# One load for the last heads' output weights in a fused decode layer: all 12 rows per partition behind the last V

## Chip, cores, metric

One core of a Trainium2 chip. The metric is the device time in microseconds; a traced execution's span is some 2 us shorter than its time. A run here means one timed execution. In the profiles PE is TensorE's matmuls and PEld its weight loads, DVE is VectorE, ACT ScalarE, POOL GpSimd, and SP the engine that issues most loads. The granted clock is the share of full speed that PE was given.

## The reference

Attention of one query position over the last 2048 cached positions, for 2 batch entries and 32 heads of 192, then a gated feed-forward layer. Almost every byte read is used once.

```python
q = (layernorm(x) @ wq)                                  # 640 -> 32 heads x 192
p = softmax(q . k_cache[:, :, 6144:, :] * 192 ** -0.5)
h = x + (p . v_cache[:, :, 6144:, :]) @ wo               # 6144 -> 640
h2 = h + (gelu(layernorm(h) @ w_gate) * (layernorm(h) @ w_up)) @ w_down
```

## The kernel before

SP issues every large load in one order into a ring of six slots; a load is issued when the work on what its bytes overlap is done. The last eight heads (J = 3) use wo in three pieces: 8 and 3 rows per partition through the ring, and the last 128 rows of wo through a separate early load `wosp` on ACT's queue, ahead of x.

```python
P.op("act", lambda e: e.dma_start(wosp[32:96, :, :], A_wo[WOE:, :].rearrange("(p j) n -> p j n", j=2)), W=["wosp"], dma="dsp")
P.op("act", lambda e: e.dma_start(xrow[0:2, :], A_x[:, 0, :]), W=["xrow"], dma="dx")
load_k(0)
load_wq()
# ... K and V of 16 groups, wo of J = 0 and 1 between them (cut)
load_wo(2)
load_wo(3)
load_ffn()                      # gate, up (2 parts), w_down (4 parts of 6, 3, 2, 1 rows)

def wo_parts(J):
    return ((0, 12),) if J < 3 else ((0, 8), (8, 11))

# the end of the program
pv(15)
o_rows(3)
oproj(2)
o_columns(3)
oproj(3)                        # wosp's rows, then 8 rows, then 3: 4 + 16 + 6 matmuls of 320 columns
h_columns()                     # then layernorm, gate, up, down
```

Of the kernel before, what the change touches and what calls it, by code (L numbers as in the profile page):

```python
# [5 lines left out]
BF16 = mybir.dt.bfloat16  # L6
F32 = mybir.dt.float32
I32 = mybir.dt.int32
ALU = mybir.AluOpType
ACT = mybir.ActivationFunctionType  # L10
AX = mybir.AxisListType

B = 2
D = 640
NC5 = D // 128
HQ = 32
DH = 192
# [198 lines left out]
RING = 6 * SLOT  # L216
TPG = 64
WDC = ((0, 6), (6, 9), (9, 11), (11, 12))
WOE = 6016
WUC = ((0, 4), (4, 5))  # L220
BIG = 1.0e9
K_AT = (0, SLOT, 3 * SLOT, 5 * SLOT)
# [6 lines left out]
def bass_sequential_preLN__sliding_block_cached__geglu_ffn__decode_kernel(  # L229
# [12 lines left out]
    with ExitStack() as ctx:  # L242

        def sb(name, shape, dt):
            return ctx.enter_context(nc.sbuf_tensor(name, shape, dt))

        def ps(name, shape, dt):
            return ctx.enter_context(nc.psum_tensor(name, shape, dt))
# [5 lines left out]
        identf = sb("identf", [128, 128], F32)  # L254
# [12 lines left out]
        selb = sb("selb", [128, 2], BF16)  # L267
# [4 lines left out]
        pf = sb("pf", [128, 11], F32)  # L272
        pg = sb("pg", [128, 13], F32)
        ci = sb("ci", [128, 128], I32)
        cti = sb("cti", [128, 4, 128], I32)
        cf = sb("cf", [128, 5, 128], F32)
        ei = sb("ei", [128, 6], I32)
        ef = sb("ef", [128, 6], F32)
        ge = sb("ge", [128, 6, 5], F32)

        wosp = sb("wosp", [128, 2, D], BF16)
        xrow = sb("xrow", [128, D], BF16)
        xT = sb("xT", [128, NC5, B], F32)
        ls = sb("ls", [128, 2, B], F32)
# [12 lines left out]
        sm = sb("sm", [128, 512], F32)  # L297
# [7 lines left out]
        ering = sb("ering", [128, 4, 32, 32], BF16)  # L305
        osb = sb("osb", [128, 384], F32)
        orow = sb("orow", [128, 8, DH], BF16)
        ot = sb("ot", [128, 13, B], BF16)
        yrow = sb("yrow", [128, 160], BF16)
        hrow = sb("hrow", [128, 320], F32)  # L310
        hsel = sb("hsel", [128, 2, 17], F32)
        grow = sb("grow", [128, 384], F32)
        urow = sb("urow", [128, 384], F32)
        gsb = sb("gsb", [128, NF * B], F32)
        ga = sb("ga", [128, 4, NF * B], F32)
        uT = sb("uT", [128, NF, 18], BF16)
# [1 line left out]
        tps = [ps(f"tps{i}", [128, 512], F32) for i in range(4)]  # L318
        sps = ps("sps", [128, 512], F32)
        ops_ = ps("ops", [128, 512], F32)  # L320
        m1 = ps("m1", [128, 512], F32)
        m2 = ps("m2", [128, 512], F32)

        P = _Prog()
# [4 lines left out]
        def load(key, off, nbytes, src, shape, sem):  # L329
            queue.append((key, off, nbytes, src, shape, sem))  # L330
# [16 lines left out]
        def done(*keys):  # L347
            used.update(keys)
            pump()
# [13 lines left out]
                 lambda v: v.rearrange("p (c n) -> p c n", n=HQ * DH), "wq")  # L363

        def load_wo(J):
            nk = 12 if J < 3 else 11
            src = A_wo[1536 * J:1536 * J + 128 * nk, :].rearrange("(p kk) n -> p kk n", kk=nk)
            for i, (k0, k1) in enumerate(wo_parts(J)):
                load(("wo", J, i), WO_AT[J] + 2 * k0 * D, 2 * (k1 - k0) * D, src[:, k0:k1, :],
                     lambda v: v.rearrange("p (kk n) -> p kk n", n=D), "wo" if J < 2 else f"wo{J}{i}")  # L370

        def wo_parts(J):
            return ((0, 12),) if J < 3 else ((0, 8), (8, 11))

        def load_ffn():
            load(("wg", 0), K_AT[1], 2 * NC5 * F, B_w_gate.rearrange("(p c) f -> p c f", c=NC5),
# [11 lines left out]
        def dve(fn, R=(), W=(), X=(), cls=1):  # L388
            return P.op("dve", fn, R, W, X, cls=cls)

        def act(fn, R=(), W=(), X=()):
            return P.op("act", fn, R, W, X)

        def pe(fn, R=(), W=(), X=()):
            return P.op("pe", fn, R, W, X)

        def pool(fn, R=(), W=(), X=()):
            return P.op("pool", fn, R, W, X)
# [7 lines left out]
        def tt(out, a, b, op):  # L406
            return lambda e: e.tensor_tensor(out=out, in0=a, in1=b, op=op)  # L407

        P.op("act", lambda e: e.dma_start(wosp[32:96, :, :], A_wo[WOE:, :].rearrange("(p j) n -> p j n", j=2)), W=["wosp"], dma="dsp")
        P.op("act", lambda e: e.dma_start(xrow[0:2, :], A_x[:, 0, :]), W=["xrow"], dma="dx")  # L410
        load_k(0)
        load_wq()
# [18 lines left out]
        pool(lambda e: e.memset(ering[:, :, :, :].rearrange("p a b c -> p (a b c)").bitcast(I32), 0), W=[("er", k) for k in range(4)])  # L431

        pool(lambda e: e.memset(uT[:, :, :].rearrange("p a b -> p (a b)").bitcast(I32), 0), W=["uT"])
        pool(lambda e: e.memset(wosp[0:32, :, :].rearrange("p a b -> p (a b)").bitcast(I32), 0), W=["wosp0"])

        dve(lambda e: e.tensor_copy(cf[:, 0, :], ci[:, :]), R=["ci"], W=["cf0"])
        dve(lambda e: e.tensor_copy(pg[:, 0:1], pi[:, :]), R=["pi"], W=["row"])
# [32 lines left out]
        def _x_T(e):  # L470
# [11 lines left out]
            R=["pi"] + [("bits", k) for k in range(11)], W=["pti"])  # L482
# [205 lines left out]
                   wm[:, :].unsqueeze(2).to_broadcast([128, 8, DH]), ALU.mult), R=["wm"], W=["orow"], X=[tok])  # L688

        def o_columns(J):  # L690
            nk = 12 if J < 3 else 11
            of = orow[:, :, :].rearrange("p h d -> p (h d)")

            def fn(e):
                for kk in range(nk):
                    ins = e.matmul(m2[:, 2 * kk:2 * kk + 2], lhsT=of[:, kk:128 * nk:nk], rhs=selb[:, :], start=True, stop=True)  # L696
                for j in range(13 - nk if J == 3 else 0):
                    ins = e.matmul(m2[0:96, 22 + 2 * j:24 + 2 * j], lhsT=of[:, 128 * nk - 64 + j:1536:2], rhs=selb[:, :], start=True,
                                   stop=True)
                return ins  # L700

            pe(fn, R=["orow", "selb"], X=["m2"])
            n = 24 if J < 3 else 26
            dve(lambda e: e.tensor_copy(ot[:, :, :].rearrange("p k b -> p (k b)")[:, 0:n], m2[:, 0:n]), W=["ot"], X=["m2"])

        def oproj(J):
            def fn_early(e):
                for j in range(2):
                    for h in range(2):
                        r = 2 * j + h  # L710
                        ins = e.matmul(m1[32 * r:32 * r + 2, 192:512], lhsT=ot[0:96, 11 + j, :], rhs=wosp[0:96, j, 320 * h:320 * (h + 1)],
                                       start=False, stop=False, tile_position=(0, 32 * r), skip_group_check=True)
                return ins

            if J == 3:
                pe(fn_early, R=["wosp", "wosp0", "ot"], X=["m1"])
            for i, (k0, k1) in enumerate(wo_parts(J)):
                wo, wtoks = where["wo", J, i]

                def fn(e, k0=k0, k1=k1, wo=wo):  # L720
                    if J == 2:
                        for h in range(2):
                            e.matmul(m1[32 * h:32 * h + 2, 192:512], lhsT=identb[0:2, 0:2], rhs=xrow[0:2, 320 * h:320 * (h + 1)],
                                     start=True, stop=False, tile_position=(0, 32 * h), skip_group_check=True)
                    for kk in range(k0, k1):
                        for h in range(2):
                            r = 2 * (kk % 2) + h
                            ins = e.matmul(m1[32 * r:32 * r + 2, 192:512], lhsT=ot[:, kk, :],  # L728
                                           rhs=wo[:, kk - k0, 320 * h:320 * (h + 1)], start=(kk == 1 or J < 2 and kk == 0) and J < 3,
                                           stop=(J < 2 and kk >= 10 or J == 3 and kk >= 9), tile_position=(0, 32 * r), skip_group_check=True)  # L730
                    return ins

                pe(fn, R=wtoks + ["ot", "xrow", "identb"], X=["m1"])
                done(("wo", J, i))
            if J == 0:
                dve(lambda e: e.tensor_copy(hrow[0:98, :], m1[0:98, 192:512]), W=["hrow"], X=["m1"])
            if J == 1:
                dve(tt(hrow[0:98, :], m1[0:98, 192:512], hrow[0:98, :], ALU.add), R=["hrow"], W=["hrow"], X=["m1"])
            if J == 3:
                dve(lambda e: e.tensor_tensor_reduce(out=hrow[0:98, :], in0=m1[0:98, 192:512], in1=hrow[0:98, :], scale=1.0, scalar=0.0,  # L740
                                                     op0=ALU.add, op1=ALU.add, accum_out=rs[0:98, :]), R=["hrow"], W=["hrow", "rs"], X=["m1"])
# [69 lines left out]
        def ffn_columns(row, tok, bank, i):  # L811
            def fn(e):
                for j in range(3):
                    ins = e.transpose(bank[:, 128 * j:128 * j + 98], row[0:98, j:384:3], identf[0:98, 0:98])
                return ins

            pe(fn, R=[tok, "identf"], X=[("t", i)])
            return bank[:, 0:384].rearrange("p (j r y) -> p r j y", j=3, y=32)[:, :, :, 0:2]

        def h_rows(e):  # L820
# [6 lines left out]
            return t.rearrange("p (r j b) -> p r j b", r=4, j=3)  # L827

        ffn_in(sps, "s", "wg", ((0, NC5),))
        dve(lambda e: e.tensor_copy(grow[0:98, :], sps[0:98, 0:384]), W=["grow"], X=["s"])  # L830
        pe(h_rows, R=["hrow", ("hsel", 0), ("hsel", 1)], X=["m1"])
        gT = ffn_columns(grow, "grow", tps[0], 0)
        dve(lambda e: e.tensor_copy(rjb(gsb[:, :]), gT), W=["gsb"], X=[("t", 0)])
        dve(tt(ga[:, 0, :], gsb[:, :], gsb[:, :], ALU.mult), R=["gsb"], W=["ga0"])
        dve(ts(ga[:, 1, :], ga[:, 0, :], 0.044715, ALU.mult, 1.0, ALU.add), R=["ga0"], W=["ga1"])
# [3 lines left out]
        dve(lambda e: e.reciprocal(ga[:, 1, :], ga[:, 3, :]), R=["ga3"], W=["ga1"])  # L839
        dve(tt(ga[:, 0, :], ga[:, 1, :], gsb[:, :], ALU.mult), R=["ga1", "gsb"], W=["ga0"])  # L840
        ffn_in(ops_, "o", "wu", WUC)
        act(lambda e: e.activation(out=urow[0:98, :], in_=ops_[0:98, 0:384], func=ACT.Copy), W=["urow"], X=["o"])
        vT = ffn_columns(urow, "urow", tps[1], 1)
        dve(tt(uT[:, :, 0:17:16].rearrange("p (r j) b -> p r j b", r=4), vT, rjb(ga[:, 0, :]), ALU.mult), R=["ga0"], W=["uT"], X=[("t", 1)])
        for i, (f0, f1) in enumerate(WDC):
            wd, wtoks = where["wd", i]

            def fn(e, f0=f0, f1=f1, wd=wd):
# [10 lines left out]
             dma="dout")  # L859
# [59 lines left out]
```

## Time and profile before

| | before |
|---|---|
| time, median of 3 (lowest to highest) | 294.46 us (294.35 to 294.63) |
| span of the traced run | 292.5 us |
| bytes moved | 122.44 MB in 6586 packets |
| mean granted PE clock | 0.857 |

The table is read together with the lines shown in the prediction below: full transfer engines, and a PE that waits for the last loads.

### The profile page before, as it was taken

How to read it: one execution, taken by the hardware profiler on the slowest of the kernel's cores; microseconds unless marked ns; L12 is line 12 of the kernel's file. 1: busy time of each engine (PE TensorE's matmuls, PEld its weight loads, DVE VectorE, ACT ScalarE, POOL GpSimd, SP SyncE). 2: the span in 40 equal slices, each digit the busy share in tenths (PEclk: the TensorE clock that was granted, in tenths of full speed). 3: DMA queues.
4: the chain of work that ended last, by engine and by line, in shares of the span. 5: the costliest groups of instructions: out<-in, count | busy, mean ns of one | idle time of the engine just before them, and what ended most of it. 6: DMA issues, size and time to landing. Idle time of an engine off the chain costs nothing.

```text
span 292.5 us, 5073 instructions
## 1 busy us (share of the span) xinstructions
PE 194.5 (66%) x2144; PEld 152.3 (52%) x2144; DVE 128.4 (44%) x310; ACT 96.2 (33%) x120; POOL 9.2 (3%) x37
## 2 busy tenths in 40 slices
PE   0248568848778198849496596759596957585674
PEld 0238356717465195628283575457566744563432
DVE  4186165623537154616155154425365554262321
ACT  1023134623442143616142153325252543341000
POOL 4000010000000000000000000000000000000000
PEclk9995989995979579998869599969797999897955
DMA  7999999999999999999999999999999999999993
GB/s 280 442 437 421 426 430 430 429 429 430 426 434 421 434 430 431 430 430 430 434 427 428 434 430 430 430 434 430 430 434 434 430 430 430 430 430 415 422 412 148
DMA packets 6586, 122.44 MB, mean 419 GB/s; under 512 B 750, under 2 KB 880, under 8 KB 1584
## 3 DMA queue, kind: packets, MB, share of 16 engines
q1 hardware_dynamic: 6480, 122.13, 97.8%
q8 instruction: 7, 0.11, 0.2%
q10 hardware_dynamic: 96, 0.17, 0.1%
q14 instruction: 3, 0.02, 0.0%
HBM read 122.29 MB, written 0.00 MB: 418 GB/s over the span
## 4 chain that ended last, share of the span: by engine, by line
DMA 77%; PE 19%; SPq 2%; DVE 1%; issue 0%
DMA ring<-in_A_k_cache_dram 57%; PE tps L558 15%; DMA ring<-in_A_wq_dram 10%; DMA ring<-in_B_w_down_dram 10%; SPq L345 2%; PE tps L579 1%; PE ops L660 1%; PE m L728 1%; PE m L696 1%; DVE ktr L570 0%; DVE ering L407 0%; PE m L851 0%; PE m L644 0%; PE m L674 0%; DVE yrow L857 0%
## 5 line engine op out<-in xcount | busy, mean ns | idle before, releaser
L558 PE MATMUL tps<-identf,ring 128*128 128x128 f32 x768 | 116.5, 321 | 46.8 <-DMA ring<-in_A_k_cache_dram 41.5
L558 PEld LDWEIGHTS tps<-identf,ring 128*128 128x128 f32 x768 | 108.1, 169 | 49.9 <-DMA ring<-in_A_k_cache_dram 42.7
L567 ACT ACTIVATE ktr<-tps 128x1024 bf16<-128x1024 bf16 x80 | 79.4, 1023 | 87.3 <-PE tps L558 87.3
L570 DVE COPY ktr<-tps 128x1024 bf16<-128x1024 bf16 x112 | 74.2, 688 | 75.1 <-PE tps L558 74.3
L635 ACT ACTIVATE eexp<-sm,nm 128x512 bf16<-128x512 f32 x16 | 11.5, 721 | 65.4 <-DVE nm L633 65.4
L660 PE MATMUL ops<-ring,ering 128*32 128x384 bf16 x512 | 25.0, 339 | 6.1 <-DMA ring<-in_A_v_cache_dram 6.1
L624 DVE CUSTOM_DVE_ANT_1 sm<-sps,mska 128x512 f32<-128x512 f32 x16 | 11.1, 692 | 36.0 <-PE sps L616 36.0
L616 PE MATMUL sps<-ktr,rq 128*16 128x512 bf16 x384 | 24.6, 388 | 1.1 <-POOL rq L407 1.1
L660 PEld LDWEIGHTS ops<-ring,ering 128*32 128x32 bf16 x512 | 12.7, 99 | 14.9 <-DMA ring<-in_A_v_cache_dram 7.6
L616 PEld LDWEIGHTS sps<-ktr,rq 128*16 128x16 bf16 x384 | 9.3, 88 | 11.4 <-POOL rq L407 1.2
L631 PEld LDWEIGHTS m<-mrhs,pm 128*128 128x128 bf16 x16 | 1.5, 96 | 23.4 <-DVE mrhs L403 23.4
L631 PE MATMUL m<-mrhs,pm 128*128 128x16 bf16 x16 | 2.9, 183 | 15.8 <-DVE mrhs L403 15.8
L407 POOL TENSOR_TENSOR rq<-qs,mask 128x96 bf16<-128x96 bf16 x16 | 5.6, 360 | 195.1 <-PE sps L616 163.4
L463 ACT ACTIVATE lt<-m,eps_t 128x2 f32<-128x2 f32 x2 | 0.5, 262 | 26.0 <-PE m L461 26.0
L407 DVE TENSOR_TENSOR ering<-m,mask 128x256 bf16<-128x256 f32 x16 | 6.7, 419 | 2.7 <-PE m L644 2.6
L472 PE MATMUL m<-identb,xrow 2*128 2x2 bf16 x5 | 0.3, 172 | 11.4 <-DMA xrow<-in_A_x_dram 11.4
L472 PEld LDWEIGHTS m<-identb,xrow 2*128 2x128 bf16 x5 | 0.3, 122 | 11.3 <-issue 11.3
L644 PE MATMUL m<-sel,eexp 128*128 128x64 bf16 x64 | 4.8, 200 | 1.2 <-ACT eexp L635 1.2
L644 PEld LDWEIGHTS m<-sel,eexp 128*128 128x128 bf16 x64 | 4.4, 105 | 1.6 <-DVE nm L633 1.3
L407 DVE TENSOR_TENSOR orow<-m,wm 128x1536 bf16<-128x1536 f32 x3 | 5.3, 1751 | 0.0
L670 DVE COPY osb<-ops 128x192 f32<-128x192 f32 x8 | 2.5, 354 | 6.0 <-PE ops L660 6.0
L696 PE MATMUL m<-selb,orow 128*128 128x2 bf16 x47 | 3.4, 199 | 1.9 <-DVE ering L407 1.6
(121 smaller groups left out, 89.0 us busy)
## 6 DMA issues: line engine op xcount, KB each, us to landing
ring<-in_A_k_cache_dram SPq DMA_DIRECT2D x16, 3072.0 KB, 32.0
ring<-in_A_v_cache_dram SPq DMA_DIRECT2D x16, 3072.0 KB, 27.4
ring<-in_A_wq_dram SPq DMA_DIRECT2D x1, 7680.0 KB, 28.7
ring<-in_A_wo_dram SPq DMA_DIRECT2D x3, 1920.0 KB, 19.5
ring<-in_B_w_gate_dram SPq DMA_DIRECT2D x1, 1920.0 KB, 31.7
ring<-in_B_w_up_dram SPq DMA_DIRECT2D x1, 1536.0 KB, 24.5
ring<-in_A_wo_dram SPq DMA_DIRECT2D x1, 1280.0 KB, 26.8
ring<-in_B_w_down_dram SPq DMA_DIRECT2D x1, 960.0 KB, 26.9
```

Source lines behind the costliest of these rows:

```text
L345: P.op("sp", lambda e, v=v, src=src: e.dma_start(v, src), W=toks + [("sem", sem)], dma=sem)
L407: return lambda e: e.tensor_tensor(out=out, in0=a, in1=b, op=op)
L558: ins = e.transpose(tps[bi][:, 128 * u:128 * (u + 1)], kv[:, off:off + 128], identf[:, :])
L567: act(lambda e, dst=dst, bv=bv: e.activation(out=dst, in_=bv, func=ACT.Copy), W=[("kt", n)], X=[("t", bi)])
L570: dve(lambda e, dst=dst, bv=bv: e.tensor_copy(dst, bv), W=[("kt", n)], X=[("t", bi)], cls=0)
L616: ins = e.matmul(sps[32 * ch:32 * ch + 16, :], lhsT=rq[:, g % 4, k, :], rhs=ktr[:, k // 2, 1024 * ch + k % 2:1024 * (ch + 1):2], start=(k ...
L624: dve(lambda e: e.tensor_tensor_reduce(out=sm[:, :].rearrange("p (u x) -> p u x", u=4), in0=sps[:, :].rearrange("p (u x) -> p u x", u=4), ...
L631: pe(lambda e: e.matmul(m2[:, 256:272], lhsT=pm[:, :], rhs=mrhs[:, :], start=True, stop=True), R=["pm", "mrhs"], X=["m2"])
L635: act(lambda e: e.activation(out=eexp[:, :], in_=sm[:, :], func=ACT.Exp, bias=nm[:, 0:1], scale=1.0, accum_out=zr[:, g % 4:g % 4 + 1]), R= ...
L644: ins = e.matmul(o, lhsT=eexp[:, 128 * u:128 * (u + 1)], rhs=sel64[:, :], start=True, stop=True)
L660: ins = e.matmul(ops_[32 * r:32 * (r + 1), 0:384], lhsT=ering[:, g % 4, t, :], rhs=vv[:, 384 * t:384 * (t + 1)], start=(g % 4 == 0 and t < 4),
L696: ins = e.matmul(m2[:, 2 * kk:2 * kk + 2], lhsT=of[:, kk:128 * nk:nk], rhs=selb[:, :], start=True, stop=True)
```

## The change

The intent: one regular load of 12 rows per partition for the last heads too, no early load with a layout of its own, and less on-chip memory.

```diff
-            src = A_wo[1536 * J:1536 * J + 128 * nk, :].rearrange("(p kk) n -> p kk n", kk=nk)
+            src = A_wo[1536 * J:1536 * (J + 1), :].rearrange("(p kk) n -> p kk n", kk=12)
...
         def wo_parts(J):
-            return ((0, 12),) if J < 3 else ((0, 8), (8, 11))
+            return ((0, 12),)
...
-        P.op("act", lambda e: e.dma_start(wosp[32:96, :, :], A_wo[WOE:, :].rearrange("(p j) n -> p j n", j=2)), W=["wosp"], dma="dsp")
         P.op("act", lambda e: e.dma_start(xrow[0:2, :], A_x[:, 0, :]), W=["xrow"], dma="dx")
...
-            if J == 3:
-                pe(fn_early, R=["wosp", "wosp0", "ot"], X=["m1"])
...
-        cti = sb("cti", [128, 4, 128], I32)
+        cti = orow[:, :, :].rearrange("p h d -> p (h d)").bitcast(I32)[:, 0:512].rearrange("p (k x) -> p k x", k=4)
-        grow = sb("grow", [128, 384], F32)
-        urow = sb("urow", [128, 384], F32)
+        grow = sm
+        urow = osb
```

Cut: the buffer of `wosp`, its memset and its matmuls (`fn_early`), the column products for the odd row count with the size of `ot`, the stop flags, and the tokens that follow from the shared buffers.

More of the change, by code (lines that the diff above doesn't have):

```diff
@@ L218 @@
 WDC = ((0, 6), (6, 9), (9, 11), (11, 12))
-WOE = 6016
 WUC = ((0, 4), (4, 5))
@@ L279, in bass_sequential_preLN__sliding_block_cached__geglu_ffn__decode_kernel @@
         ge = sb("ge", [128, 6, 5], F32)
-        wosp = sb("wosp", [128, 2, D], BF16)
         xrow = sb("xrow", [128, D], BF16)
@@ L307, in bass_sequential_preLN__sliding_block_cached__geglu_ffn__decode_kernel @@
         orow = sb("orow", [128, 8, DH], BF16)
-        ot = sb("ot", [128, 13, B], BF16)
+        cti = orow[:, :, :].rearrange("p h d -> p (h d)").bitcast(I32)[:, 0:512].rearrange("p (k x) -> p k x", k=4)
+        ot = sb("ot", [128, 12, B], BF16)
         yrow = sb("yrow", [128, 160], BF16)
@@ L365, in load_wo @@
         def load_wo(J):
-            nk = 12 if J < 3 else 11
-            src = A_wo[1536 * J:1536 * J + 128 * nk, :].rearrange("(p kk) n -> p kk n", kk=nk)
+            src = A_wo[1536 * J:1536 * (J + 1), :].rearrange("(p kk) n -> p kk n", kk=12)
             for i, (k0, k1) in enumerate(wo_parts(J)):
@@ L433, in bass_sequential_preLN__sliding_block_cached__geglu_ffn__decode_kernel @@
         pool(lambda e: e.memset(uT[:, :, :].rearrange("p a b -> p (a b)").bitcast(I32), 0), W=["uT"])
-        pool(lambda e: e.memset(wosp[0:32, :, :].rearrange("p a b -> p (a b)").bitcast(I32), 0), W=["wosp0"])
         dve(lambda e: e.tensor_copy(cf[:, 0, :], ci[:, :]), R=["ci"], W=["cf0"])
@@ L690, in o_columns @@
         def o_columns(J):
-            nk = 12 if J < 3 else 11
-            of = orow[:, :, :].rearrange("p h d -> p (h d)")
             def fn(e):
-                for kk in range(nk):
-                    ins = e.matmul(m2[:, 2 * kk:2 * kk + 2], lhsT=of[:, kk:128 * nk:nk], rhs=selb[:, :], start=True, stop=True)
-                for j in range(13 - nk if J == 3 else 0):
-                    ins = e.matmul(m2[0:96, 22 + 2 * j:24 + 2 * j], lhsT=of[:, 128 * nk - 64 + j:1536:2], rhs=selb[:, :], start=True,
-                                   stop=True)
+                for kk in range(12):
+                    ins = e.matmul(m2[:, 2 * kk:2 * kk + 2], lhsT=orow[:, :, kk:DH:12], rhs=selb[:, :], start=True, stop=True)
                 return ins
             pe(fn, R=["orow", "selb"], X=["m2"])
-            n = 24 if J < 3 else 26
-            dve(lambda e: e.tensor_copy(ot[:, :, :].rearrange("p k b -> p (k b)")[:, 0:n], m2[:, 0:n]), W=["ot"], X=["m2"])
+            dve(lambda e: e.tensor_copy(ot[:, :, :].rearrange("p k b -> p (k b)"), m2[:, 0:24]), W=["ot"], X=["m2"])
         def oproj(J):
-            def fn_early(e):
-                for j in range(2):
-                    for h in range(2):
-                        r = 2 * j + h
-                        ins = e.matmul(m1[32 * r:32 * r + 2, 192:512], lhsT=ot[0:96, 11 + j, :], rhs=wosp[0:96, j, 320 * h:320 * (h + 1)],
-                                       start=False, stop=False, tile_position=(0, 32 * r), skip_group_check=True)
-                return ins
-            if J == 3:
-                pe(fn_early, R=["wosp", "wosp0", "ot"], X=["m1"])
             for i, (k0, k1) in enumerate(wo_parts(J)):
@@ L729, in fn @@
                                            rhs=wo[:, kk - k0, 320 * h:320 * (h + 1)], start=(kk == 1 or J < 2 and kk == 0) and J < 3,
-                                           stop=(J < 2 and kk >= 10 or J == 3 and kk >= 9), tile_position=(0, 32 * r), skip_group_check=True)
+                                           stop=(J != 2 and kk >= 10), tile_position=(0, 32 * r), skip_group_check=True)
                     return ins
@@ L815, in fn @@
                 return ins
-            pe(fn, R=[tok, "identf"], X=[("t", i)])
+            pe(fn, R=[*tok, "identf"], X=[("t", i)])
             return bank[:, 0:384].rearrange("p (j r y) -> p r j y", j=3, y=32)[:, :, :, 0:2]
@@ L829, in bass_sequential_preLN__sliding_block_cached__geglu_ffn__decode_kernel @@
         ffn_in(sps, "s", "wg", ((0, NC5),))
-        dve(lambda e: e.tensor_copy(grow[0:98, :], sps[0:98, 0:384]), W=["grow"], X=["s"])
+        dve(lambda e: e.tensor_copy(grow[0:98, 0:384], sps[0:98, 0:384]), W=["sm"], X=["s"])
         pe(h_rows, R=["hrow", ("hsel", 0), ("hsel", 1)], X=["m1"])
-        gT = ffn_columns(grow, "grow", tps[0], 0)
+        gT = ffn_columns(grow, ["sm"], tps[0], 0)
         dve(lambda e: e.tensor_copy(rjb(gsb[:, :]), gT), W=["gsb"], X=[("t", 0)])
@@ L841, in bass_sequential_preLN__sliding_block_cached__geglu_ffn__decode_kernel @@
         ffn_in(ops_, "o", "wu", WUC)
-        act(lambda e: e.activation(out=urow[0:98, :], in_=ops_[0:98, 0:384], func=ACT.Copy), W=["urow"], X=["o"])
-        vT = ffn_columns(urow, "urow", tps[1], 1)
+        act(lambda e: e.activation(out=urow[0:98, :], in_=ops_[0:98, 0:384], func=ACT.Copy), W=[("osb", 0), ("osb", 1)], X=["o"])
+        vT = ffn_columns(urow, [("osb", 0), ("osb", 1)], tps[1], 1)
         dve(tt(uT[:, :, 0:17:16].rearrange("p (r j) b -> p r j b", r=4), vT, rjb(ga[:, 0, :]), ALU.mult), R=["ga0"], W=["uT"], X=[("t", 1)])
```

## The prediction

> **What bounds the kernel now.** I read the page first: which engine is full, in which slices of the span, and what the chain that ended last is made of.
>
> ```profile
> PE 194.5 (66%) x2144; PEld 152.3 (52%) x2144; DVE 128.4 (44%) x310; ACT 96.2 (33%) x120; POOL 9.2 (3%) x37
> ...
> DMA  7999999999999999999999999999999999999993
> ...
> q1 hardware_dynamic: 6480, 122.13, 97.8%
> q8 instruction: 7, 0.11, 0.2%
> q10 hardware_dynamic: 96, 0.17, 0.1%
> ...
> DMA 77%; PE 19%; SPq 2%; DVE 1%; issue 0%
> ```
>
> No compute engine is over 66%. The transfer engines are at 9 tenths in every slice but the first and the last, and the packets of the SP queue alone fill 97.8% of 16 engines' span. 0.978 x 292.5 us is 286 us of solid transfer, so only about 6.5 us lie outside it: the start and the finish. Where the chain names PE in the middle, it names what released a later load. It doesn't show an idle queue.
>
> Next the stretches of those two ends: length, busy time of PE, PEld, DVE, ACT and POOL, then granted clock, transfer share and GB/s.
>
> ```profile
> 0.00:2.00 2.00, 0.00 (x0) 0.00 (x0) 0.84 (x3) 0.00 (x0) 1.38 (x19) 1.00 0.00 0
> 2.00:10.00 8.00, 0.00 (x0) 0.00 (x0) 2.19 (x5) 1.28 (x1) 2.13 (x3) 1.00 1.03 414
> 10.00:250.00 240.00, 165.93 (x1802) 134.29 (x1802) 111.90 (x265) 87.83 (x108) 5.65 (x16) 0.87 1.00 430
> 260.00:286.00 26.00, 17.72 (x235) 9.09 (x223) 7.95 (x28) 2.20 (x7) 0.00 (x0) 0.76 0.99 417
> 286.00:288.00 2.00, 1.30 (x23) 1.00 (x27) 0.22 (x1) 0.34 (x1) 0.00 (x0) 0.50 0.77 301
> 288.00:290.00 2.00, 1.75 (x40) 0.58 (x28) 0.00 (x0) 0.00 (x0) 0.00 (x0) 0.50 0.20 72
> ```
>
> Nothing moves for 2 us, then the engines are full until 286 us, then they finish unevenly. The order of time, from the last heads on, shows who waits for whom there.
>
> ```profile
> 274.03 0.31 PE L711 MATMUL m<-wosp,ot 96*2 96x320 bf16 x4 [0.28 <-DVE ot L704]
> 274.51 0.71 PE L728 MATMUL m<-ring,ot 128*2 128x320 bf16 x16 [0.17 <-DMA ring<-in_A_wo_dram]
> 275.74 0.44 PE L728 MATMUL m<-ring,ot 128*2 128x320 bf16 x6 [0.51 <-DMA ring<-in_A_wo_dram]
> ...
> 284.02 0.10 PEld L805 LDWEIGHTS ops<-ring,hnT 128*2 128x2 bf16 x8 [0.32 <-DMA ring<-in_B_w_up_dram]
> ...
> 287.46 0.65 PEld L851 LDWEIGHTS m<-ring,uT 128*17 128x17 bf16 x24 [0.61 <-DVE uT L407]
> 288.46 0.25 PEld L851 LDWEIGHTS m<-ring,uT 128*17 128x17 bf16 x12 [0.34 <-DMA ring<-in_B_w_down_dram]
> 289.25 0.12 PEld L851 LDWEIGHTS m<-ring,uT 128*17 128x17 bf16 x8 [0.55 <-DMA ring<-in_B_w_down_dram]
> 289.66 0.10 PEld L851 LDWEIGHTS m<-ring,uT 128*17 128x17 bf16 x4 [0.29 <-DMA ring<-in_B_w_down_dram]
> ```
>
> PE waits for both parts of the last wo (8 rows per partition, then 3), a little for up, and for three of the four parts of w_down. The last part landed at about 289.6 us; four matmuls, one copy and the output's transfer follow. The end is the landing of the last byte plus a fixed 3 us.
>
> **What the Trainium skill says.** "DMA: Bandwidth & Descriptors", section "Issuing engines are not separate DMA queues", states that transfers issued from any engine run on the same 16 transfer engines and interleave. So the separate load of wo rows (wosp, 160 KB on ACT's queue) is no free lane. The trace agrees: it took 9.5 us from issue to landing beside the first K load, where 160 KB at 430 GB/s would be 0.38 us.
>
> The same page, "Queues, rings and completion order", says that each transfer engine takes turns between queues packet by packet. The trace's transfer records agree: wosp's 64 packets go in four rounds about 1.0 us apart between K packets of 24576 B, and x, issued behind them on ACT's queue, comes in the next round. That is why the first use of x starts at 11.36 us.
>
> The same page, "Why small descriptors are slow (HBM only)", gives each packet a fixed overhead. The median packet times in the trace show its size: 0.055 us for 1280 B, 0.102 for 2560, 0.149 for 3840, 0.389 for 10240, 0.578 for 15360, 0.915 for 24576. The slope between first and last is 0.0369 us per 1000 B, which leaves about 8 ns per packet. A completion packet takes 9 ns.
>
> "TensorE: Matmul & The Clock Gate", Part 1, says the PE clock is throttled by default and that activity releases it. Here it was 1.00 from 271 to 277 us and 0.50 from 277 on, which matters for the rival below.
>
> **The change, part by part.** I work per transfer engine; there are 16, and a load over 128 partitions gives each 8 packets.
>
> (1) Taken away at the start: wosp, 4 packets of 0.102 us and one completion, 0.417 us. K0, wq and all behind them come 0.42 us earlier.
>
> (2) Changed near the end: the last wo was 8 x 0.389 + 8 x 0.149 and two completions, 4.32 us; it becomes 8 x 0.578 and one completion, 4.63 us: +0.31 us.
>
> (3) The sum is -0.11 us per engine. Every byte is still read, only in 192 fewer data packets and 32 fewer completions. As the queue is always full, this sum moves the last landing, from 289.6 to about 289.5 us.
>
> (4) SP has one issue less (0.43 us). It issued the w_down parts between 260 and 270 us, some 20 us ahead of their landing, so this is worth nothing.
>
> (5) x goes first on ACT's queue and should land near 6 us rather than 11.3. Layernorm and the first K transposes start earlier. But the q projection waits for wq (start 30.31 us), so I expect 0.4 us there, only what (1) gives; no loading follows from more.
>
> (6) PE near the end. The four wosp matmuls go (0.31 us), and two narrow column products become one; both ended before the wait for wo. In exchange all 24 wo matmuls start after the whole load has landed, where only 6 did. The 24 of the previous heads took 0.99 us from 271.64, the 6 took 0.44: +0.55 us. The wo load ends 0.11 us earlier, so the residual row is 0.44 us later, and so are layernorm and gate. Up then loses only what its wait doesn't absorb: PE's transposes before it ended their weight loads at 283.70, up waited until 284.02 for its weights. So up starts at about 284.15, uT is ready about 0.13 us later, near 287.55. The 44 down matmuls before the last four need 44 x 28 ns (0.65 us for 23 steps), 1.23 us, so they can end at 288.8. The last w_down lands at 289.5. Hidden, with 0.7 us to spare.
>
> (7) gate and up rows in the buffers of the softmax scores and of the head outputs: their last readers ran by 264.6 and 271.0 us, gate is written at 282.6 and up at 285.85. The wait lists of both built kernels show no added semaphore on those two copies. The integer constants in the head rows' buffer are DVE writing and reading before the heads exist. POOL loses one memset of 0.62 us at 3.5 us, which nothing waited for. Each is worth zero.
>
> Sum: -0.11 us, 294.46 to 294.35.
>
> **The rivals.** *PE becomes the bound.* In the new kernel PE idles about 2 us before the 24 wo matmuls. If that drops the clock to 0.50 there, their 0.69 us of steps doubles: another 0.7 us, uT near 288.25, the down matmuls ready for the last part at 289.5, just as it lands. I make that at most +0.3 us, 294.7. For it: the clock does fall from 277. Against: two stacked losses are needed to use up the slack.
>
> *Fewer transfers save their fixed cost.* If each load cost its own latency in line, two loads fewer would give 2 us or more, about 292. Against: packets of consecutive loads follow without a hole, share 0.99 from 260 to 286.
>
> *The start gives more than the end takes.* If loads had been issued late because compute was late, earlier x and wq would close holes. At 97.8% there are hardly any; at most -0.4 us, 294.05.
>
> *Uneven finish.* The transfer records of the last load fall into two bunches: 72 packets done by 298.7 on the records' own clock, 56 between 299.2 and 300.2. That is nine engines and seven, and there are seven instruction fetches of about 1.04 us. My reading, not shown, is that each fetch sets one engine back. A shorter program may move a fetch, and two on one engine would cost about 1 us: 295.4; one fewer would hardly help while six remain.
>
> **Range and chances.** The known sum is a tenth of a microsecond, below the spread of the three runs of before (294.35 to 294.63). I add the PE rival and rounding upward and put the prediction at 294.4. The range covers the start's gain and normal variation downward, the fetch and clock rivals in part upward: 293.6 to 295.3. Two per cent is 5.9 us; neither side has anything of that size.
>
> **What would show it.** The SP queue with 128 packets and one 16-packet completion fewer, and 80 packets (wosp's 64 and 16) gone from ACT's; solid share as before; first use of x near 6 us; q projection near 29.9 us; one group of 24 wo matmuls starting near 275.6; up starting near 284.1 with less or no wait; still a wait for w_down before the last matmuls. I am wrong if that last wait is gone, if the share shows a hole, or if the last landing moves by more than a microsecond.

## More of the kernel before

One more line of the page says what the chain that ended last is made of, by engine and line.

```profile
DMA ring<-in_A_k_cache_dram 57%; PE tps L558 15%; DMA ring<-in_A_wq_dram 10%; DMA ring<-in_B_w_down_dram 10%; SPq L345 2%; PE tps L579 1%; PE ops L660 1%; PE m L728 1%; PE m L696 1%; DVE ktr L570 0%; DVE ering L407 0%; PE m L851 0%; PE m L644 0%; PE m L674 0%; DVE yrow L857 0%
```

Its last load is w_down, 10% of the span, and the work of PE on it (L851) is next to nothing.

## The result and the profile after

| | before | after |
|---|---|---|
| time, median of 6 | 294.43 us | 294.51 us |
| lowest to highest | 294.33 to 294.63 | 293.85 to 294.88 |
| ratio, 95% interval | | 1.0001 (0.9986 to 1.0015) |
| span of the traced run | 292.5 us | 292.8 us |

A ratio is the mean time of one kernel's runs over that of the other's in the same rounds, so not quite the ratio of the medians. The median stays, but the six runs are 293.85, 294.17, 294.19 and 294.84, 294.86, 294.88: two groups with nothing between, where the kernel before varied by 0.3 us. The trace below is of a run at 294.86, so of the slower group. First the page's lines.

```profile
PE 197.3 (67%) x2141; PEld 153.7 (52%) x2141; DVE 128.3 (44%) x310; ACT 96.2 (33%) x120; POOL 8.6 (3%) x36
...
DMA  7998999999999999999999999999999999999993
...
q1 hardware_dynamic: 6336, 122.29, 97.8%
...
q10 hardware_dynamic: 16, 0.01, 0.0%
...
DMA 71%; PE 24%; SPq 1%; DVE 1%; issue 1%; ACT 0%
DMA ring<-in_A_k_cache_dram 52%; PE tps L553 16%; DMA ring<-in_A_wq_dram 10%; DMA ring<-in_A_wo_dram 9%; PE tps L574 2%; SPq L343 1%; PE m L706 1%; PE ops L655 1%; PE m L829 1%; PE sps L783 1%; PE ops L783 1%; PE m L688 1%; PE tps L792 1%; PE m L725 0%; DVE ering L404 0%
```

The queues are as predicted: 144 packets fewer for SP, 80 fewer for ACT. The chain is not. w_down has gone from it; its last load is wo, and from there it runs through the compute of the whole feed-forward part (L725, L783, L792, L829).

The same stretches as before (length, PE, PEld, DVE, ACT, POOL busy, clock, transfer share, GB/s):

```profile
10.00:250.00 240.00, 167.49 (x1793) 133.53 (x1793) 108.36 (x244) 86.97 (x105) 5.63 (x16) 0.84 1.00 430
260.00:286.00 26.00, 16.57 (x208) 9.12 (x204) 7.29 (x25) 1.28 (x4) 0.00 (x0) 0.69 1.00 422
...
288.00:290.00 2.00, 1.69 (x49) 1.45 (x48) 0.22 (x1) 0.00 (x0) 0.00 (x0) 0.50 0.14 52
```

The transfers are as full as before and finish, if anything, slightly earlier (52 instead of 72 GB/s in the last stretch). The time line of the end shows the rest.

```profile
275.47 1.77 PE L706 MATMUL m<-ring,ot 128*2 128x320 bf16 x24 [2.37 <-DMA ring<-in_A_wo_dram]
277.29 0.49 DVE L718 CUSTOM_DVE_ANT_0 hrow<-m,hrow 98x320 f32<-98x320 f32 x1 [3.98 <-PE m L706]
...
285.03 1.77 PE L783 MATMUL ops<-ring,hnT 128*2 128x384 bf16 x20
...
288.46 1.45 PEld L829 LDWEIGHTS m<-ring,uT 128*17 128x17 bf16 x48 [0.61 <-DVE uT L404]
...
290.29 0.33 DVE L835 CAST yrow<-m 113x160 bf16<-113x160 f32 x1 [1.89 <-PE m L829]
```

All 24 wo matmuls start at 275.47, close to the predicted 275.6, but take 1.77 us. The residual row follows at 277.29 (276.22 before), uT (the feed-forward activations that w_down is multiplied with) is ready at 288.41, and then all 48 loads of weights for down run in one piece, "x48", where the kernel before had stops for three parts of w_down. Nothing waits for w_down any more, which the prediction had named as a sign of being wrong, and the output's copy starts at 290.29 instead of 290.03.

### The profile page after: what moved, and what is told of

The parts are those of the page before. It is cut to its first block, busy times and chain, and to the rows that moved or that the text cites. A ratio compares the mean times of both kernels' runs of the same rounds, so it can differ in the third digit from the quotient of the medians.

```text
span 292.8 us, 5063 instructions
## 1 busy us (share of the span) xinstructions
PE 197.3 (67%) x2141; PEld 153.7 (52%) x2141; DVE 128.3 (44%) x310; ACT 96.2 (33%) x120; POOL 8.6 (3%) x36
## 4 chain that ended last, share of the span: by engine, by line
DMA 71%; PE 24%; SPq 1%; DVE 1%; issue 1%; ACT 0%
DMA ring<-in_A_k_cache_dram 52%; PE tps L553 16%; DMA ring<-in_A_wq_dram 10%; DMA ring<-in_A_wo_dram 9%; PE tps L574 2%; SPq L343 1%; PE m L706 1%; PE ops L655 1%; PE m L829 1%; PE sps L783 1%; PE ops L783 1%; PE m L688 1%; PE tps L792 1%; PE m L725 0%; DVE ering L404 0%
## 5 line engine op out<-in xcount | busy, mean ns | idle before, releaser
L553 PEld LDWEIGHTS tps<-identf,ring 128*128 128x128 f32 x768 | 106.8, 168 | 46.8 <-DMA ring<-in_A_k_cache_dram 43.9
L611 PE MATMUL sps<-ktr,rq 128*16 128x512 bf16 x384 | 26.0, 405 | 1.1 <-POOL rq L404 1.1
L574 PE MATMUL tps<-ring,xnT 128*32 128x384 bf16 x80 | 5.8, 478 | 10.8 <-DMA ring<-in_A_wq_dram 10.8
L574 PEld LDWEIGHTS tps<-ring,xnT 128*32 128x32 bf16 x80 | 3.3, 138 | 13.2 <-issue 11.0
L597 DVE CAST qs<-ops 128x384 bf16<-128x384 f32 x1 | 0.6, 558 | 17.6 <-PE ops L592 17.6
L706 PE MATMUL m<-ring,ot 128*2 128x320 bf16 x96 | 4.7, 340 | 2.4 <-DMA ring<-in_A_wo_dram 2.4
L581 ACT ACTIVATE qrow<-tps 128x768 bf16<-128x768 f32 x1 | 0.8, 810 | 15.6 <-PE tps L574 15.6
```

The source lines that it names most:

```text
L553: ins = e.transpose(tps[bi][:, 128 * u:128 * (u + 1)], kv[:, off:off + 128], identf[:, :])
L574: ins = e.matmul(tps[0][32 * r:32 * (r + 1), 0:384], lhsT=xnT[:, c, 32 * J:32 * (J + 1)], rhs=wq[:, c, 1536 * J + 384 * r:1536 * J + 384 * ...
L611: ins = e.matmul(sps[32 * ch:32 * ch + 16, :], lhsT=rq[:, g % 4, k, :], rhs=ktr[:, k // 2, 1024 * ch + k % 2:1024 * (ch + 1):2], start=(k ...
L706: ins = e.matmul(m1[32 * r:32 * r + 2, 192:512], lhsT=ot[:, kk, :], rhs=wo[:, kk - k0, 320 * h:320 * (h + 1)], start=(kk == 1 or J < 2 and ...
```

## The experiments

Theory A: the transfers end about 0.1 us earlier, but with 24 matmuls behind the last wo byte PE has hardly any time to spare; in runs where the clock granted there is 0.50, these matmuls take 0.8 us longer, PE sets the end, and the run is slow. Theory B: the transfers themselves end differently from run to run. Ten experiments were run, two of them the changed kernel unedited, in three batches on three chips; each batch had its own 9 runs of the kernel before, with medians 294.35, 294.34 and 294.35.

### 1. The changed kernel again

Edit: none, twice.

> The changed kernel, not edited, to see its two groups of times again (294.2 and 294.86 so far) with the clock of each run. Theory A (PE clock): the runs fall into two groups again, about 294.1 with a whole-run clock of 0.85 to 0.88 and about 294.85 with 0.82 to 0.83; the mean over all is within 0.2% of before. Theory B (transfers end differently from run to run): a spread without relation to the clock.

> The changed kernel once more, unedited, to count how many of its runs are in the slow group (5 of 11 so far, by a span of 292.7 us or more). Theory A: between a quarter and three quarters of these runs again, none of them in between; the rest near 294.05.

Measured: 294.11, 294.48, 293.94, 294.86, 293.99 (ratio 0.9998), and in the later batch 295.16, 294.58, 294.31, 295.01, 294.13 (ratio 1.0006, interval 0.9992 to 1.0019). The first time, the traced run was one of the quick ones (294.11). Its time line:

```profile
275.65 1.09 PE L706 MATMUL m<-ring,ot 128*2 128x320 bf16 x24 [2.45 <-DMA ring<-in_A_wo_dram]
276.78 0.49 DVE L718 CUSTOM_DVE_ANT_0 hrow<-m,hrow 98x320 f32<-98x320 f32 x1 [3.36 <-PE m L706]
...
284.51 1.77 PE L783 MATMUL ops<-ring,hnT 128*2 128x384 bf16 x20
...
287.94 1.32 PEld L829 LDWEIGHTS m<-ring,uT 128*17 128x17 bf16 x44 [0.61 <-DVE uT L404]
...
289.50 0.10 PEld L829 LDWEIGHTS m<-ring,uT 128*17 128x17 bf16 x4 [0.24 <-DMA ring<-in_B_w_down_dram]
289.87 0.33 DVE L835 CAST yrow<-m 113x160 bf16<-113x160 f32 x1 [1.98 <-PE m L829]
```

Same kernel, same start of the wo matmuls within 0.2 us, but 1.09 us for them instead of 1.77, and then a last wait of 0.24 us for w_down. So the last bytes set the end of this run. The clock of the two runs in stretches of 1 us, first the slow run (294.86), then the quick one (294.11); the granted clock is the third number from the end:

```profile
273.00:274.00 1.00, 0.10 (x2) 0.01 (x1) 0.18 (x1) 0.00 (x0) 0.00 (x0) 0.71 0.90 384
275.00:276.00 1.00, 0.53 (x12) 0.30 (x16) 0.00 (x0) 0.00 (x0) 0.00 (x0) 0.50 1.15 476
276.00:277.00 1.00, 1.00 (x20) 0.36 (x12) 0.00 (x0) 0.00 (x0) 0.00 (x0) 0.50 0.86 369
```

```profile
273.00:274.00 1.00, 0.20 (x4) 0.11 (x2) 0.18 (x1) 0.00 (x0) 0.00 (x0) 1.00 0.90 384
275.00:276.00 1.00, 0.35 (x12) 0.30 (x16) 0.00 (x0) 0.00 (x0) 0.00 (x0) 1.00 1.01 415
276.00:277.00 1.00, 0.74 (x20) 0.21 (x12) 0.22 (x1) 0.00 (x0) 0.00 (x0) 0.71 1.01 430
```

In the slow run the clock falls at about 273.4, ahead of the matmuls, in the quick one at about 276.4, behind most of them. In the later batch's traced run (295.16) it was 0.50 already in the stretch from 268 to 269 us, and stayed there; nothing waited for w_down in it either. These are the only two slow runs with a trace. The clock of a whole run is a poor label, against the expectation: a run at 0.840 took 294.86, one at 0.848 took 293.94. The span is a better one. Of all 16 runs of the changed kernel, 8 have a span of 292.0 to 292.3 us (mean time 294.09) and 8 of 292.6 to 293.1 (mean 294.83). Two of those, 294.48 and 294.58, lie in between in time, which I had not expected. Of the 27 runs of the kernel before in the three batches, one has a span over 292.4 (292.8, at 294.56); it has no trace.

### 2. Keep the clock up during the wait

```diff
+        def warm(n):     # n matmuls of 512 columns into an unused bank
...
         pv(15)
+        warm(1)
         o_rows(3)
         oproj(2)
+        warm(1)
         o_columns(3)
+        warm(5)
         oproj(3)
```

> The changed kernel with 7 idle matmuls of 512 columns into an unused bank, 1 and 1 before the last head columns and 5 in the 2.3 us wait for the last wo. Theory A: the clock stays at 1.00 until the 24 wo matmuls, these take about 1.0 us (1.77 in the profiled run of the changed kernel), PE waits for w_down again at the end, and the slow group is gone: all runs 294.0 to 294.3. Theory B: two groups as before, no change of the median (294.5).

Measured: 293.98, 294.20, 294.21, 294.36, 294.47, all spans 292.0 to 292.4; ratio 0.9997.

```profile
272.85 1.24 PE L735 MATMUL tps<-ktr,identb 128*128 128x512 bf16 x5
275.38 0.99 PE L706 MATMUL m<-ring,ot 128*2 128x320 bf16 x24 [1.30 <-DMA ring<-in_A_wo_dram]
...
289.27 0.10 PEld L840 LDWEIGHTS m<-ring,uT 128*17 128x17 bf16 x4 [0.29 <-DMA ring<-in_B_w_down_dram]
```

The clock was 1.00 from 271 to 277, the 24 matmuls took 0.99 us, PE waited for w_down again, and no run has a long span. Two of the runs are above the range that I gave; with five runs I don't read more into 0.2 us.

### 3. Split the load again, without the early one

```diff
-            return ((0, 12),)
+            return ((0, 12),) if J < 3 else ((0, 8), (8, 12))
```

> The changed kernel with its last wo in two loads, 8 and 4 rows per partition. Theory A: only 8 of the 24 matmuls are left after the last byte, so the half clock costs some 0.3 us instead of 0.8: slow group gone, all runs about 294.2 (transfers 0.1 us longer than in the changed kernel by packet sizes). Theory B: two groups as before, median 294.6.

Measured: 294.06, 294.07, 294.29, 294.30, 294.43, spans 292.1 to 292.4; ratio 0.9994. The trace happens to have the clock at 0.50 during wo, which makes it the sharper test:

```profile
274.08 2.00 PE L706 MATMUL m<-ring,ot 128*2 128x320 bf16 x24 [0.28 <-DVE ot L692]
275.38 0.10 PEld L706 LDWEIGHTS m<-ring,ot 128*2 128x2 bf16 x8 [0.67 <-DMA ring<-in_A_wo_dram]
276.14 0.49 DVE L718 CUSTOM_DVE_ANT_0 hrow<-m,hrow 98x320 f32<-98x320 f32 x1 [2.11 <-PE m L706]
```

Sixteen of the matmuls run before the last rows land; at half the clock the residual row is still at 276.14, 1.15 us ahead of the slow run of the changed kernel, and the end waits for w_down. The clock was 1.00 again from 285.5 to 288.9, which helped the end of this run, but not the residual row. Here a low clock cost little, since most of the work lay ahead of the last byte.

### 4. The kernel before, with its 11 rows in one load

```diff
-            return ((0, 12),) if J < 3 else ((0, 8), (8, 11))
+            return ((0, 12),) if J < 3 else ((0, 11),)
```

> The kernel before with the 11 rows of its last wo in one load, the early load of the two other rows kept. Theory A: 22 matmuls behind the last byte, so the slow group of the changed kernel appears here too: some runs near 294.7, some near 294.3. Theory B, or a theory that the moved rows or the earlier x make the two groups: one group at 294.3 to 294.5, as before.

Measured: 294.97, 294.48, 294.38, 294.19, 294.17; spans 292.9 for the first, 292.1 to 292.4 for the others; ratio 0.9997. The traced run is the long one:

```profile
275.59 1.76 PE L728 MATMUL m<-ring,ot 128*2 128x320 bf16 x22 [0.53 <-DMA ring<-in_A_wo_dram]
...
288.56 1.45 PEld L851 LDWEIGHTS m<-ring,uT 128*17 128x17 bf16 x48 [0.61 <-DVE uT L407]
...
290.39 0.32 DVE L857 CAST yrow<-m 113x160 bf16<-113x160 f32 x1 [1.89 <-PE m L851]
```

The signature of the changed kernel's slow runs, with the early rows and the late x of the kernel before still in place. One run in five is too few for a rate, or to differ from the one in 27 of the kernel before; what counts is the trace, in which 22 matmuls at clock 0.50 lie behind the last byte and nothing waits for w_down. The cause thus needs neither the moved rows nor the earlier x: merging the load is enough.

### 5. x ahead of the early rows, in the kernel before

```diff
-        P.op("act", ... wosp ...)
         P.op("act", ... xrow ...)
+        P.op("act", ... wosp ...)
```

> The kernel before with the load of x issued ahead of the early load of wo rows. If x was late only because it stood behind those rows in its queue, its first use moves from 11.4 us to about 4 us. Since the first layernorm and K transposes end long before wq lands, the time stays: 294.2 to 294.5, ratio 1.000. Rival (earlier x lets loads be issued earlier): 294.0 or less.

Measured: 294.13, 294.25, 294.36, 294.46; ratio 0.9996 (0.9981 to 1.0012). x's first use is at 4.28 us instead of 11.36. Nothing follows for the time. A side effect that I had missed: PE is now idle for 10.76 us before wq lands, and the q projection takes 6.26 us instead of 3.43, with a clock of 0.54 over it instead of 1.00, so the next K is issued at 36.40 instead of 33.79. The same is seen in the changed kernel, ahead of it the kernel before:

```profile
30.31 3.43 PE L579 MATMUL tps<-ring,xnT 128*32 128x384 bf16 x80 [1.50 <-DMA ring<-in_A_wq_dram]
```

```profile
29.64 5.80 PE L574 MATMUL tps<-ring,xnT 128*32 128x384 bf16 x80 [10.81 <-DMA ring<-in_A_wq_dram]
```

It costs nothing, since a K and a V load of 3072 KB each are still to come when the projection begins at 30.09, an estimated 14.6 us of transfer at the 430 GB/s of the stretch from 10 to 250 us; the issue at 36.40 falls well within them.

### 6. The 160 KB put back as dead freight

```diff
+        P.op("act", lambda e: e.dma_start(spare[32:96, :, :], A_wo[6016:, :].rearrange("(p j) n -> p j n", j=2)), W=["spare"], dma="dsp")
```

It goes behind x, into a buffer that nobody uses (the last wo matmuls carry a wait for it, long met).

> The changed kernel with the early load of the two wo rows put back as dead freight (160 KB on the second queue behind x, into a buffer that nobody uses). If every byte at the start is paid at the end, the last w_down lands 0.42 us later (4 packets of 0.102 us and a completion on each transfer engine): the fast group 294.1 becomes 294.5, the slow one 294.85 becomes 295.2. Rival (the early load fills a hole at the start and is free): no change.

Measured: 294.47, 294.51, 294.56 and 295.10, 295.25; ratio 1.0017 (1.0003 to 1.0031). The mean of the quick three is 294.51, that of the changed kernel's quick eight 294.09: +0.42 us, the predicted price of the bytes; the two slow ones are 0.34 us over the slow eight. So in this kernel bytes read in the first microseconds were paid at the end, and the early load was not free. That it agrees to the hundredth is luck, with three runs picked by their time. The comparison is across batches, but each batch's own kernel before has the same median within 0.01 us.

The traced run (294.47, one of the quick three) shows one thing more:

```profile
275.88 1.77 PE L708 MATMUL m<-ring,ot 128*2 128x320 bf16 x24 [1.58 <-issue]
...
289.36 0.11 PEld L831 LDWEIGHTS m<-ring,uT 128*17 128x17 bf16 x8 [0.35 <-DMA ring<-in_B_w_down_dram]
```

Its 24 wo matmuls ran at clock 0.50, as in the slow runs, and the residual row came at 277.70, later than in either slow trace of the changed kernel. But the clock was 1.00 from 286.2 on, the first 36 weight loads for down took 0.60 us, and PE waited for w_down again. So a half clock at the wo matmuls does not make a run slow by itself; the work that follows must run at a half clock too.

### 7. The wo matmuls twice

```diff
+                if J == 3:
+                    pe(again, R=wtoks + ["ot"], X=[("t", 3)])     # the same 24 matmuls into an unused bank
                 pe(fn, R=wtoks + ["ot", "xrow", "identb"], X=["m1"])
```

> The changed kernel with the 24 wo matmuls of the last heads done twice, the first time into an unused bank. Theory A (PE sets the end once the wo matmuls are late): the spare time of about 0.25 us that was left in the run at full clock is used up: at full clock +0.7 us of matmuls gives 294.5 to 294.7, at half clock +1.25 us gives about 296; no wait for w_down is left. Theory B (the transfers set the end in every run): 294.1 to 294.9 as the changed kernel.

Measured: 294.35, 295.10, 295.24, 296.10; ratio 1.0028 (1.0006 to 1.0050). In the traced run (295.24) the two sets took from 275.43 to 278.80 at clock 0.50, uT was ready at 289.75, and the 48 down matmuls ran without a stop, in 1.01 us, as the clock had risen again. The range of 1.75 us between the runs is more than the two values that I expected. One run (294.35) lies in theory B's 294.1 to 294.9, and three lie above it. In the traced one, what PE does after the last wo byte sets the time, at twice the weight here.

### 8. Both cures together

Edit: the splits of experiment 3 and the idle matmuls of experiment 2.

> The changed kernel with both cures, wo in loads of 8 and 4 rows and the 7 idle matmuls. Theory A: PE waits for w_down with some 0.8 us to spare, one group of times at 294.0 to 294.4, no better than the split alone, since the transfers set the end: the gain over before is at most 0.2 us.

Measured: 294.23, 294.25, 294.30, 294.33, 294.41; ratio 0.9998 (0.9985 to 1.0012). One narrow group, and no gain: with PE out of the way the transfers set the end, as in the kernel before. With experiments 2 and 3 that makes 15 runs of cured kernels without one span over 292.4, against 8 of 16 above it in the changed kernel. None of the versions beats both kernels clearly.

### 9. The buffers alone, in the kernel before

Edit: the lines of the change for `cti`, `grow` and `urow`, with their tokens.

> The kernel before with the buffers of the change alone: integer constants in the head rows' buffer, gate and up rows in those of the scores and head outputs; all loads as before. If the buffers are worth nothing, as predicted, the time is that of before, 294.2 to 294.5, with one group. Rival (a copy waits for an old reader of the shared buffer, or the other addresses change a rate): a later uT, or over 0.3 us of difference.

Measured: 294.29, 294.29, 294.38, 294.46; ratio 0.9999 (0.9984 to 1.0015). uT is ready at 287.22, against 287.41 before. The buffers are worth nothing in time.

## Why the prediction was right, and where it was not

The total was right: 294.4 predicted, 294.51 measured, inside 293.6 to 295.3. That it came so close is partly luck: it is the middle of two groups, one below and one above, which the prediction treated as a main case and an unlikely rival. Of its signs of being wrong, one came true in the result's own trace: the last wait for w_down was gone.

**The transfers, (1) to (3).** Predicted: 0.42 us taken away at the start, 0.31 added near the end, -0.11 in sum. Experiment 6 supports the first term, with +0.42. The quick half of the changed kernel's runs has a mean of 294.09, 0.26 us under the common median of the three batches' kernel before (294.35). That is more than 0.11; the quick half was picked by its span, which biases it downward. The transfer records fit the small sum better: the last packet of w_down ends at 289.18, 288.97 and 289.01 us in the traces of the kernel before and of experiments 5 and 9, whose loads are the same, and at 288.81, 289.01 and 289.11 in the three of the changed kernel, so 0.08 us earlier in the mean, but with a spread of 0.2 to 0.3 among equal loads. They show no more than the predicted 0.11, and are too few to rule more out. (The prediction's "landed at about 289.6" is when PE's wait ended, 0.48 us behind the last packet; in the quick run it is 0.49, so this drops out.)

**SP and x, (4) and (5).** Right for the time (experiment 5). x's first use came at 3.75 us, not 6; the trace puts the wait before it down to a constant of DVE, so x was there even earlier than I had estimated. (In the kernel before x came one round of packets later than the prediction says: wosp's completions took the round in between, at 9.5 to 9.9 us, and x followed at 10.5.) The q projection began at 29.64 as against 29.9 predicted. That it would run at a lower clock was not foreseen, and had no effect.

**PE near the end, (6).** This is the step that failed: "Hidden, with 0.7 us to spare". In the slow runs nothing was hidden, and even in the quick run the spare time was 0.24 us, since the 44 loads of weights that began at 287.94 took 1.32 us, and the last four waited until 289.50. The term that was mis-sized most is the wait of up. I had taken the end of the transposes' weight loads, 283.70, as the time from which up waited until 284.02, so 0.3 us would be absorbed. But in the quick run, where up waits for nothing, it starts 0.69 us after the transposes do (283.82 to 284.51); in the kernel before that would have been 283.24 + 0.69 = 283.93. Only 0.09 us was there to absorb. A residual row 0.56 us later (276.78 for 276.22) thus became a uT 0.48 us later (287.89 for 287.41), not 0.13. Two smaller misses add up with it: the 24 matmuls took 1.09 us and not 0.99, as the clock fell within them, and the 44 weight loads took 0.09 us more than the 1.23 predicted.

**The clock rival.** From the half clock on its mechanism was right, but the idling before the matmuls, to which it put the drop down, can hardly be the reason in the slow traces: the clock fell 0.3 us after PE had stopped in one (273.09 to 273.42) and 6 us before PE stopped in the other (267.68). Its chance was wrong: 8 of 16 runs, by their spans, not a remote stack of two losses. With 0.24 us to spare while the end runs at half clock, one loss is enough. The size was also low: I allowed "at most +0.3 us" for a uT near 288.25; measured were 288.41 in the first trace and 288.73 in the slowest traced run, and the slow half's mean is 0.48 us over the kernel before. The Trainium skill, "TensorE: Matmul & The Clock Gate", Part 1, says that the window over which activity is judged runs freely and does not reset when a kernel starts. The traces fit this. In all twelve, every stretch from one change of the clock to the next lasts a whole multiple of 3.41 us, and the last fall came at 273.42, 276.41 and 267.68 us in three runs of one program: these are no multiples of 3.41 apart, so the steps begin at another point in each run. That this phase is what sorts the runs is my reading; no run here controls it. Experiments 2, 3 and 4 settle only the next link: in the traces the end was lost to PE where the 24 (or 22) matmuls lay behind the last byte at a half clock that lasted to the end, and the long runs went when the load was split or the clock kept up. Experiment 6's trace shows that the half clock at these matmuls alone does not suffice.

**The buffers, (7).** Right (experiment 9).

**The other rivals.** No fixed cost per load was saved, and no hole at the start was closed: experiment 6 finds the early bytes at their full price. The uneven finish is the same in both kernels (7 instruction fetches each, and in the transfer records of the changed kernel's first trace again 72 packets of the last load in an early bunch and 56 in a late one); whether the fetches cause it was not tested.

So the net against the kernel before is: half of the runs 0.26 us quicker, of which the prediction explains 0.11, and the other half 0.48 us slower, with PE at a low clock as the cause in the two that were traced.

## What to carry to other kernels

In this kernel, with transfers full from end to end, moving bytes between an early and a late load left the sum as it was; only packets and completions were saved. What can be lost is the overlap at the end: a load that is split lets most of the dependent matmuls run before its last rows land, and how much that is worth must be judged at the lowest clock that PE may get there, not at the one that one trace shows. Absorbed waits should be measured from when the waiting work could have started, taken from a run where it does not wait.

## What the Trainium skill lacked or had wrong

- "DMA: Bandwidth & Descriptors", "Why small descriptors are slow (HBM only)", gives the fixed cost per packet in bus cycles, and the page states no time per packet for loads that SP or ACT issue. The packet times here give one: 0.055 us for 1280 B to 0.915 us for 24576 B, so about 8 ns per packet, and 9 ns per completion.
- The same page, "Where 436 GB/s comes from", says that for transfers from HBM the limit of about 358 GB/s binds, a memory stack's bandwidth divided by two cores. With one core at work this kernel moved 430 GB/s from 10 to 250 us, close to the page's other limit of 435. The fact is not lacking, since the same section reports 425 GB/s for one transfer of 16 MB; the sentence alone misleads.
- "TensorE: Matmul & The Clock Gate", Part 1, names a busy window but not how busy it must be. In the kernel before PE was busy in 10.04 of the 15 us from 277 to 292 us, with small matmuls, and the granted clock was 0.50 throughout.
- The same page explains variation from run to run by where a kernel's first matmul falls in the window; the drops of the clock that it describes inside a kernel come at every wait of a loop. Here runs differ at the end of a program of 290 us: the same 24 matmuls took 1.09 us in one run and 1.77 us in another, and the slow half of the runs is 0.74 us behind the quick half (294.83 and 294.09). As a share of the span, 0.3%, this stays below the 1% that the page gives for a ramp.
